# Linear attention with an MLP: far chunks' projections in small PE tiles, and a planner that counts a lead for each run of small operations

## The chip, the cores and the metric

The kernel runs on one core of one Trainium2 chip. The metric is the device time of one execution in microseconds; smaller is better. Three runs of the kernel before took 245.31, 246.84 and 247.11 us, so the median is 246.84 us.

## What is computed

Inputs are float32. The attention is linear: each head's query and key vector x (32 values) becomes 64 features, the products of all pairs of S1 x and S2 x. Its output, laid out as 4352 tokens of 128 values, goes through an MLP with 2048 hidden columns.

```python
def phi(x):
    a = np.einsum('rd,bhsd->bhsr', S1, x)
    b = np.einsum('rd,bhsd->bhsr', S2, x)
    return np.einsum('bhsi,bhsj->bhsij', a, b).reshape(*x.shape[:-1], r * r)
q_p, k_p = (phi(q), phi(k))
kv = np.einsum('bhsf,bhsd->bhfd', k_p, v)
z = np.sum(k_p, axis=2)
num = np.einsum('bhsf,bhfd->bhsd', q_p, kv)
den = np.einsum('bhsf,bhf->bhs', q_p, z)[..., None] + 1e-06
...
h = x @ w_in
g = h * np.clip(h + 3.0, 0.0, 6.0) / 6.0
out = g @ w_out
```

There are 4 batches, 4 heads, 1088 positions and r = 8.

## The kernel before, in words

The tokens are cut into eight chunks of 512 and a last one of 256 (CHUNKS), which gathers the last 64 positions of all batches. The hidden columns are cut into eight pairs of 128-column blocks (fp 0 to 7).

Keys (`keys`, `features`): for each batch two groups of tiles are projected on PE (abps_k, L530), copied by ACT (ab_k, L539) and multiplied to features by DVE and POOL (ph_k, L558). PE then sums features times values into one bank (kvps, L593), and ACT copies that to kvb (L618).

Queries: chunks 0 and 1 are the near ones and are turned by PE. Chunks 2 to 8 are the far ones (`far_queries`). Their projection (mm_far, L535, abps_q) takes two matmuls over 64 columns of weights each and writes one bank. DVE turns it in blocks of 32 (cp_far, L543), POOL makes the features (ph_q), DVE turns them (pht, L745), four DMAs write them to DRAM (phd, L751), and one reads them back with features across the partitions (phT, L756). PE multiplies by kvb (nd, L636) and DVE divides (L643 to L647). The result x is turned on its way through DRAM in the same manner (L773 to L782), and split into two halves xh and xl (L681, L685).

MLP: one step is a chunk c and a pair fp. h is the sum of three products for each of two blocks (L811, L812, L817), six matmuls of 512 columns. ACT makes relu (L825), DVE the gate (L828), ACT the upper half gh (L832) and POOL or DVE the lower half gl (L836). The output o is again six matmuls (L857, L858 from gh, L860 from gl). A matmul of 512 columns is called a slot below. h has two buffers, and a third step's h can be written only when the gate of the step two before has read its own. Weights come as 64-bit values and are converted in blocks of 512 columns (wi and wo 0 to 3, L371 to L396), seven steps of each on DVE.

What sets the order: each operation is entered in a `Plan` with its cost on each engine that can run it, a due time, its needs and its buffers. `Plan.order` walks through time, starts on each free engine the operation that is due first among those whose needs and buffers are there, and the instructions are emitted in that order. The due times come from the tables at the head (STEP, DUES, LAG, W_DUE, CONV_LEAD, LEADS). Each engine then executes its list in order and waits at an instruction whose needs are not there. While nothing is at hand before 17 us, fillers (warm, L354) are put in PE's list.

`bufs` of an operation are taken when it starts. Tag "a" stands for two banks that the far projections use:

```python
far_queries(c, xneed[c], ("a",), ("a",), both)
```

Of the kernel before, what the change touches and what calls it, by code (L numbers as in the profile page):

```python
# [23 lines left out]
HP = P // 2  # L24
Q = P // 4
# [8 lines left out]
AB = 2 * H * R  # L34
# [15 lines left out]
NEAR = 2  # L50
# [48 lines left out]

STEP = 5.06  # L100
DUES = (317.92, 316.34, 129.31, 384.08)
LAG = 128.57
W_DUE = (-152.92, 321.22, 23.24, 201.42, 251.62, 14.82, 266.57, 276.24)
CONV_LEAD = (-252.29, -232.94, 463.37, -221.73, 549.89, 31.5, 265.14, 219.73, 219.47)
LOAD_DUE = {}
LEADS = ({'ab': -466.98, 'cp': -244.73, 'ph': 113.36, 'kv': -102.29, 'kvb': -199.83, 'tr': -78.56, 'trcp': -30.35, 'nd': -572.11, 'norm': 297.56, 'xt': 543.02, 'xh': -868.0, 'xl': 204.57, 'k0': -407.3, 'kld': 146.8, 'vld': -256.29, 'qld': -79.85, 'rd': -154.99, 'xw': 402.82, 'xr': 513.46}, {'ab': 106.42, 'cp': 408.81, 'ph': 46.58, 'kv': 85.72, 'kvb': -43.81, 'tr': -441.07, 'trcp': -288.36, 'nd': -2.3, 'norm': -121.67, 'xt': 347.83, 'xh': 86.64, 'xl': 378.1, 'k0': 9.14, 'kld': 371.66, 'vld': 59.77, 'qld': 218.44, 'rd': 139.58, 'xw': 405.77, 'xr': 51.94}, {'ab': -161.26, 'cp': -355.61, 'ph': 225.14, 'kv': -82.13, 'kvb': 258.9, 'tr': -84.99, 'trcp': -282.18, 'nd': 9.09, 'norm': 441.52, 'xt': -380.46, 'xh': -96.54, 'xl': -168.68, 'k0': 149.54, 'kld': -6.91, 'vld': 496.37, 'qld': 447.25, 'rd': -88.95, 'xw': -359.0, 'xr': 167.27})


HOLD = 10.14
HOLD_DUE = -34.33  # L110
SOON = 0.51
SOON_DUE = 27.65
PATIENCE = 0.0
# [35 lines left out]
class Plan:  # L149
# [4 lines left out]

    def add(self, cost, due, deps, emit, bufs=(), cols=0, ready=0.0, moved=0.0, dual=False, recs=0):
        deps = [d for d in deps if d is not None]
        op = Op(cost, due, emit, list(bufs), cols, len(deps), ready, dual=dual, moved=moved, recs=recs)
        for d in deps:
            d.then.append(op)
        for b in op.bufs:  # L160
            b.left += 1
        self.ops.append(op)
        return op

    def fetched(self, t, recs):
# [32 lines left out]
    def choose(self, op, t, at, soon):  # L198
# [16 lines left out]
        return idle[0]  # L215

    def order(self):
        self.cols = {}
        self.port = 0.0
        self.begun, self.asked = 0, []  # L220
        self.moving = MOVING
# [6 lines left out]
        while left:  # L228
# [13 lines left out]
            for op in avail:  # L242
                if op.ready > t and len(op.cost) == 1 and all(b.held or any(free[g] for g in b.tags) for b in op.bufs):
                    soon[next(iter(op.cost))].append((op.ready, op.due))
            began = []
            for op in avail:
                if op.ready > t or not all(b.held or any(free[g] for g in b.tags) for b in op.bufs):
                    continue
# [77 lines left out]
def fused_kernel(ctx: ExitStack, tc: tile.TileContext, qT, kT, v1, sb, w_in, w_out, outT):  # L326
# [9 lines left out]
    def bank(tag, name):  # L336
        return psum[tag].tile([P, 512], F32, name=name, tag=tag)
# [179 lines left out]
    def features(src, n, name, tag, due, ld, srcb, psb, eng_cost, LEAD, far=False, w=HP):  # L517
# [4 lines left out]
        pb, abb, phb = Buf(psb), Buf(("ab",)), Buf((tag,))  # L522
        T["abb"], T["n"] = abb, n

# [35 lines left out]
        if far:  # L560
            o1 = plan.add({PE: 0.1 + 0.121 * n}, due - LEAD["ab"], [ld], mm_far, [srcb, pb, abb], 256 * n, S_READY, recs=8)
            o2 = plan.add({DVE: 0.12 + 0.067 * n}, due - LEAD["cp"], [o1], cp_far, [pb, abb])
        else:
            o1 = plan.add({PE: 0.13 + 0.115 * n if w == HP else 0.137 + 0.112 * n}, due - LEAD["ab"], [ld], mm, [srcb, pb, abb], 256 * n, S_READY, recs=8 * n if w == HP else 16 * n)
            o2 = plan.add({ACT: 0.06 + 0.0535 * n}, due - LEAD["cp"], [o1], cp, [pb, abb])
# [11 lines left out]
    def keys(b, due, psbs, ph_eng):  # L577
# [25 lines left out]
        for half in range(2):  # L603
# [20 lines left out]
    def divided(c, due, T, t, m, ready, phTb, nb, xb, LEAD):  # L624
# [102 lines left out]
    def far_queries(c, due, psb, ndb, ph_eng):  # L727
# [218 lines left out]
```

## Time and profile before

| what | us |
|---|---|
| median of 3 runs | 246.84 |
| lowest and highest | 245.31, 247.11 |
| the profiled execution | 244.85 |
| span of its instructions | 243.0 |
| PE busy in the span | 233.8 |
| DVE busy in the span | 184.7 |
| ACT busy in the span | 164.5 |
| POOL busy in the span | 154.1 |

The profile is of one execution, whose own time is 1.85 us longer than the span from its first to its last instruction. Times in the rows count from the start of the span. The records of matmuls overlap: a slot lasts about 0.39 us, but the next one starts earlier, so what a slot costs is read from starts. A float32 matmul leaves two records; 128*64 behind MATMUL is the size of the weights, the shape behind it is weights' or moving operand's as the profile names it. An x with a number counts records that follow each other.

### The profile page before, as it was taken

The page shows a single profiled execution, that of the slowest core. Times are in us where ns is not written, and L with a number is a line of the kernel's source. Part 1 is how long each engine was busy: PE and PEld are TensorE (multiplying, and loading weights), DVE is VectorE, ACT ScalarE, POOL GpSimd, SP SyncE. Part 2 cuts the span into 40 slices and gives each one's busy share as a digit, 9 for nine tenths or more (in the row PEclk, how much of TensorE's full clock was granted, in tenths as well). Part 3 has the DMA queues.
Part 4 walks back from the last instruction along what each step waited for, and adds up shares of the span by engine and source line. Part 5 has one row for each costly group of instructions (what it writes and reads, how often), then busy time and mean ns, then how long its engine had stood idle before and what let it go on. Part 6 is the DMA issues. An engine that isn't in the chain of part 4 may idle for free.

```text
span 243.0 us, 5464 instructions
## 1 busy us (share of the span) xinstructions
PE 233.8 (96%) x2214; PEld 182.2 (75%) x2214; DVE 184.7 (76%) x246; ACT 164.5 (68%) x205; POOL 154.1 (63%) x102
## 2 busy tenths in 40 slices
PE   8969789999999999999999899999999999999994
PEld 3757666787777778877878687777888878888894
DVE  2869999999899899788657756857648883747643
ACT  3455476888697648756766866849857875878571
POOL 2742867999699998474879844035663305867441
PEclk9999999999999999999999999999999999999999
DMA  6889973032037559704423000000100010001010
GB/s 206 263 282 386 373 249 115 1 88 87 4 87 184 180 146 295 239 0 136 127 89 86 18 29 20 25 0 3 43 0 0 0 43 3 0 0 46 0 43 22
DMA packets 18007, 23.80 MB, mean 98 GB/s; under 512 B 1728, under 2 KB 11072, under 8 KB 17984
## 3 DMA queue, kind: packets, MB, share of 16 engines
q1 hardware_dynamic: 17984, 23.48, 30.5%
q8 instruction: 17, 0.28, 0.5%
q14 instruction: 6, 0.05, 0.1%
HBM read 16.26 MB, written 7.21 MB: 97 GB/s over the span
## 4 chain that ended last, share of the span: by engine, by line
PE 86%; POOL 5%; issue 2%; DMA 2%; ACT 2%; DVE 1%; POOLq 0%; ACTq 0%
PE h L811 13%; PE o L857 13%; PE o L860 13%; PE h L817 12%; PE h L812 12%; PE o L858 12%; PE nd L636 3%; DMA woraw<-w_out_dram 2%; POOL gl L836 2%; PE warm L354 2%; PE kvps L593 2%; POOL ph_k L558 2%; PE abps_k L530 2%; PE abps_q L535 1%; PE xps L664 1%
## 5 line engine op out<-in xcount | busy, mean ns | idle before, releaser
L836 POOL TENSOR_TENSOR gl<-g,gh 128x1024 fp32r<-128x1024 f32 (+1 forms) x50 | 117.9, 2368 | 63.0 <-ACT gh L832 36.9
L828 DVE SCALAR_TENSOR_TENSOR g<-g,h 128x1024 f32<-128x1024 f32 (+1 forms) x72 | 82.9, 1156 | 24.7 <-ACT g L825 24.1
L825 ACT ACTIVATE g<-h 128x1024 f32<-128x1024 f32 (+1 forms) x72 | 70.3, 979 | 40.7 <-POOL gl L836 20.9
L832 ACT CAST gh<-g 128x1024 fp32r<-128x1024 f32 (+1 forms) x72 | 71.5, 1001 | 15.0 <-PE o L858 10.6
L811 PE MATMUL h<-xh,wi_hi 128*128 128x512 f32 (+1 forms) x148 | 56.8, 384 | 0.9 <-DVE g L828 0.9
L817 PE MATMUL h<-xl,wi_hi 128*128 128x512 f32 (+1 forms) x148 | 56.0, 378 | 0.0
L812 PE MATMUL h<-xh,wi_lo 128*128 128x512 f32 (+1 forms) x148 | 55.7, 376 | 0.0
L857 PE MATMUL o<-gh,wo_hi 128*128 128x512 f32 (+1 forms) x144 | 55.6, 389 | 0.0
L858 PE MATMUL o<-gh,wo_lo 128*128 128x512 f32 (+1 forms) x144 | 54.6, 382 | 0.0
L860 PE MATMUL o<-gl,wo_hi 128*128 128x512 f32 (+1 forms) x144 | 43.4, 385 | 0.0
L836 DVE TENSOR_TENSOR gl<-g,gh 128x1024 fp32r<-128x1024 f32 (+1 forms) x22 | 31.6, 1438 | 14.6 <-PE o L860 8.5
L811 PEld LDWEIGHTS h<-xh,wi_hi 128*128 128x128 f32 x148 | 27.7, 187 | 8.5 <-DVE g L828 1.3
L817 PEld LDWEIGHTS h<-xl,wi_hi 128*128 128x128 f32 x148 | 27.7, 187 | 5.9
L857 PEld LDWEIGHTS o<-gh,wo_hi 128*128 128x128 f32 x144 | 27.0, 188 | 6.7 <-issue 0.6
L812 PEld LDWEIGHTS h<-xh,wi_lo 128*128 128x128 f32 x148 | 27.8, 188 | 5.2
L858 PEld LDWEIGHTS o<-gh,wo_lo 128*128 128x128 f32 x144 | 27.0, 188 | 5.4
L860 PEld LDWEIGHTS o<-gl,wo_hi 128*128 128x128 f32 x144 | 25.8, 188 | 5.7 <-issue 0.4
L558 POOL TENSOR_TENSOR ph_k<-ab_k 128x512 f32<-128x512 f32 (+1 forms) x14 | 13.4, 978 | 10.9 <-ACT ab_k L539 10.9
L558 POOL TENSOR_TENSOR ph_q<-ab_q 128x512 f32<-128x512 f32 x15 | 15.8, 1073 | 0.9 <-ACT ab_q L539 0.5
L636 PEld LDWEIGHTS nd<-kvb,phT 128*32 128x32 f32 (+1 forms) x480 | 8.6, 113 | 4.0 <-issue 3.3
L593 PEld LDWEIGHTS kvps<-v,ph_k 128*32 128x32 f32 (+3 forms) x504 | 7.3, 113 | 5.4 <-issue 3.4
L593 PE MATMUL kvps<-v,ph_k 128*32 128x33 f32 (+3 forms) x504 | 8.8, 202 | 2.1 <-issue 1.6
(77 smaller groups left out, 165.8 us busy)
## 6 DMA issues: line engine op xcount, KB each, us to landing
phd<-pht SPq DMA_DIRECT2D x24, 128.0 KB, 3.9
phT<-phd SPq DMA_DIRECT2D x6, 512.0 KB, 4.4
wiraw<-w_in_dram SPq DMA_DIRECT2D x4, 512.0 KB, 5.5
qT<-qT_dram SPq DMA_DIRECT2D x8, 256.0 KB, 5.5
woraw<-w_out_dram SPq DMA_DIRECT2D x4, 512.0 KB, 5.4
outT_dram<-os SPq DMA_DIRECT2D x8, 256.0 KB, 2.0
xd<-xt SPq DMA_DIRECT2D x24, 64.0 KB, 1.8
xT<-xd SPq DMA_DIRECT2D x6, 256.0 KB, 2.7
```

Of the source, the lines that this page charges most:

```text
L558: engines[e].tensor_tensor(out, a_, b_, op=ALU.mult)
L593: nc.tensor.matmul(K["ps"][e : e + k, w], T["ph"][:rows, t, h * F + f : h * F + f + k], vbox[0][:rows, t, w], start=i == 0 and h < 2, stop ...
L811: nc.tensor.matmul(T["h"][:, u, i:j_], wi_hi[:, f], x, start=True, stop=False)
L812: nc.tensor.matmul(T["h"][:, u, i:j_], wi_lo[:, f], x, start=False, stop=False)
L817: nc.tensor.matmul(T["h"][:, u, i:j_], wi_hi[:, f], x, start=False, stop=True)
L825: nc.scalar.activation(T["g"][:, :, :n], T["h"][:, :, :n], AF.Relu, bias=3.0, scale=1.0)
L828: nc.vector.scalar_tensor_tensor(T["g"][:, :, :n], T["g"][:, :, :n], 6.0, T["h"][:, :, :n], op0=ALU.min, op1=ALU.mult)
L832: nc.scalar.copy(T["gh"][:, :, :n], T["g"][:, :, :n])
L836: engines[e].tensor_tensor(T["gl"][:, :, :n], T["g"][:, :, :n], T["gh"][:, :, :n].bitcast(F32), op=ALU.subtract)
L857: nc.tensor.matmul(o, wo_hi[:, f], T["gh"][:, u, :n], start=first and u == 0, stop=False)
L858: nc.tensor.matmul(o, wo_lo[:, f], T["gh"][:, u, :n], start=False, stop=False)
L860: nc.tensor.matmul(o, wo_hi[:, f], T["gl"][:, u, :n], start=False, stop=last and u == 1)
```

## The change

The far projection is done in eight matmuls instead of two. Each takes 64 rows (one pair of heads, p) and 32 columns of weights (that pair's), and moves a quarter g of the chunk's tokens, 128 columns. The eight tiles differ in their rows p and in the output partitions g, and the two pairs of heads write two different banks. So an operation now takes two banks of tag "a" at once, and `room` tests that two are free. DVE turns the two banks one after the other, each half as wide. Since the quarters lie otherwise in the features, each far chunk writes them with eight DMAs of half the size.

In the planner, small operations have a kind and a lead, which is counted once for a run of operations of one kind, and the costs of the small operations are lower by it. The tables of due times are all new, and with them the order of all engines. The cut diff:

```diff
-STEP = 5.06
-DUES = (317.92, 316.34, 129.31, 384.08)
+STEP = 4.32
+DUES = (370.39, 363.67, 175.22, 475.38)
...
+    lead: float = 0.0
+    kind: str = ""
...
+    def taken(self, op):
+
+        cost = op.cost[PE] + (op.lead if op.kind != self.last else 0.0)
+        self.last = op.kind
+        return cost
...
+    def room(op, free):
+
+        taken = []
+        for b in op.bufs:
+            if not b.held:
+                g = next((g for g in b.tags if free[g] > taken.count(g)), None)
+                if g is None:
+                    return False
+                taken.append(g)
+        return True
...
-                op.end = at[e] = self.run(self.fetched(t, op.recs), op.cost[e], op.cols) if e == PE else t + op.cost[e]
+                op.end = at[e] = self.run(self.fetched(t, op.recs), self.taken(op), op.cols) if e == PE else t + op.cost[e]
...
+        pbs = [pb, Buf(psb)]
...
         def mm_far(_):
-            T["ps"] = bank(pb.tag, f"abps_{name}")
-            for e in (0, HP):
-                nc.tensor.matmul(T["ps"][e : e + HP, : n * HP], s_sb, src[0][:, e * n : (e + HP) * n], start=True, stop=True)
+
+            T["pss"] = [bank(b.tag, f"abps_{name}_{p}") for p, b in enumerate(pbs)]
+            w = n * Q
+            for p, g in product(range(2), range(4)):
+                r = slice(p * HP, (p + 1) * HP)
+                nc.tensor.matmul(
+                    T["pss"][p][g * Q : (g + 1) * Q, :w],
+                    s_sb[r, p * Q : (p + 1) * Q],
+                    src[0][r, g * w : (g + 1) * w],
+                    start=True,
+                    stop=True,
+                    tile_position=(p * HP, g * Q),
+                )
...
         def cp_far(_):
             T["ab"] = buf("ab", [P, 5 * AB], f"ab_{name}")
-            nc.vector.transpose(T["ab"][:, : n * AB], T["ps"][:, : n * AB])
+            w = n * Q
+            for p in range(2):
+                nc.vector.transpose(T["ab"][:, p * w : (p + 1) * w], T["pss"][p][:, :w])
...
-            o1 = plan.add({PE: 0.1 + 0.121 * n}, due - LEAD["ab"], [ld], mm_far, [srcb, pb, abb], 256 * n, S_READY, recs=8)
-            o2 = plan.add({DVE: 0.12 + 0.067 * n}, due - LEAD["cp"], [o1], cp_far, [pb, abb])
+            o1 = plan.add({PE: 0.055 * n}, due - LEAD["ab"], [ld], mm_far, [srcb, *pbs, abb], 128 * n, S_READY, recs=32, lead=0.16, kind="far")
+            o2 = plan.add({DVE: 0.22 + 0.067 * n}, due - LEAD["cp"], [o1], cp_far, [*pbs, abb])
...
         def wr(_):
             d = dram.tile([2, 4, Q, n], F32, name=f"phd_{c}", tag=f"phd_{c}")
-            for e, p in product(range(2), range(2)):
-                k = (2 * e + p) * Q
-                nc.sync.dma_start(d[p, :, :, e * n // 2 : (e + 1) * n // 2].rearrange("f r x -> r f x"), T["turn"][k : k + Q])
+            w = n // 4
+            for g in range(4):
+                src = T["turn"][g * Q : (g + 1) * Q].rearrange("r f (p x) -> r f p x", p=2)
+                for p in range(2):
+                    nc.sync.dma_start(d[p, :, :, g * w : (g + 1) * w].rearrange("f r x -> r f x"), src[:, :, p])
...
-        a = plan.add({SP: 4 * ISSUE}, due - LEAD["trcp"], [a], wr, [turnb], moved=n * 1.024)
+        a = plan.add({SP: 8 * ISSUE}, due - LEAD["trcp"], [a], wr, [turnb], moved=n * 1.024)
```

The other small operations get lead and kind in the same manner (ab 0.135, kv 0.11, nd 0.135).

How the instructions move, at three places. Names: cva are conversion steps, wi1 is weight block 1, g_0_1 is the gate of chunk 0, pair 1.

DVE, before, around the first gates of the MLP:

```order
L396 TENSOR_TENSOR wi_lo_161<-rest_wi1_534,cva_wi1_448 128x512
L685 TENSOR_TENSOR xl_1_663<-xps_1_638,xh_1_662 128x512
L375 TENSOR_SCALAR cva_wo1_735<-woraw1_321 128x512
L828 SCALAR_TENSOR_TENSOR g_0_0_551<-g_0_0_551,h_0_0_433 128x1024
L378 SCALAR_TENSOR_TENSOR cva_wo1_735<-woraw1_321,cva_wo1_735 128x512
L543 STREAM_TRANSPOSE ab_q4_764<-abps_q4_739 128x256
L828 SCALAR_TENSOR_TENSOR g_0_1_692<-g_0_1_692,h_0_1_650 128x1024
```

and now:

```order
L397 TENSOR_SCALAR cva_wi2_694<-wiraw2_439 128x512
L397 TENSOR_SCALAR cva_wo1_701<-woraw1_322 128x512
L400 SCALAR_TENSOR_TENSOR cva_wi2_694<-wiraw2_439,cva_wi2_694 128x512
L400 SCALAR_TENSOR_TENSOR cva_wo1_701<-woraw1_322,cva_wo1_701 128x512
L864 SCALAR_TENSOR_TENSOR g_0_0_691<-g_0_0_691,h_0_0_649 128x1024
L406 TENSOR_SCALAR cva_wi2_694<-wiraw2_439 128x512
L592 TENSOR_TENSOR ph_k7_773<-abps_k7_669,ab_k7_703 128x256
L406 TENSOR_SCALAR cva_wo1_701<-woraw1_322 128x512
L409 SCALAR_TENSOR_TENSOR cva_wi2_694<-wiraw2_439,cva_wi2_694 128x512
L409 SCALAR_TENSOR_TENSOR cva_wo1_701<-woraw1_322,cva_wo1_701 128x512
L412 SCALAR_TENSOR_TENSOR wi_hi_160<-mag_wi2_652,cva_wi2_694 128x512
L864 SCALAR_TENSOR_TENSOR g_0_1_753<-g_0_1_753,h_0_1_698 128x1024
```

Ahead of the first gate there are now two conversion steps of two blocks each; between the first and the second gate stand six operations where two stood.

PE, before, from the end of h of chunk 0, pair 1, to the first product of chunk 1 (kvps_2: batch 2):

```order
L817 MATMUL h_0_1_650<-xl_0_426,wi_hi_160 128x256
L593 MATMUL kvps_2_674<-v_4_430,ph_k4_660 32x33 x16
L530 MATMUL abps_k5_695<-s_ab_157,kT_5_380 32x2x32 x20
L593 MATMUL kvps_2_674<-v_4_430,ph_k4_660 32x33 x16
L535 MATMUL abps_q4_739<-qT_4_401,s_sb_146 64x256 x2
L593 MATMUL kvps_2_674<-v_5_493,ph_k5_745 32x33 x8
L811 MATMUL h_1_0_761<-xh_1_662,wi_hi_160 128x512
L812 MATMUL h_1_0_761<-xh_1_662,wi_lo_161 128x512
```

and now:

```order
L847 MATMUL h_0_1_698<-xh_0_422,wi_hi_160 128x256
L848 MATMUL h_0_1_698<-xh_0_422,wi_lo_161 128x256
L853 MATMUL h_0_1_698<-xl_0_423,wi_hi_160 128x256
L627 MATMUL kvps_2_717<-v_4_510,ph_k4_647 32x33 x32
L627 MATMUL kvps_2_717<-v_5_394,ph_k5_584 32x33 x16
L847 MATMUL h_1_0_783<-xh_1_658,wi_hi_160 128x512
L848 MATMUL h_1_0_783<-xh_1_658,wi_lo_161 128x512
```

Between the two there is only kvps; the projections of k5 and of chunk 4 that stood there are elsewhere: k5 (and k7) ahead, chunk 4 behind.

PE, before, at a far projection:

```order
L817 MATMUL h_1_2_879<-xl_1_663,wi_hi_160 128x512
L860 MATMUL o_0_0_835<-gl_0_1_829,wo_hi_162 128x512 x2
L535 MATMUL abps_q6_895<-qT_6_628,s_sb_146 64x256 x2
L811 MATMUL h_1_3_899<-xh_1_662,wi_hi_160 128x512
L812 MATMUL h_1_3_899<-xh_1_662,wi_lo_161 128x512
```

and now, at another one:

```order
L848 MATMUL h_1_1_856<-xh_1_658,wi_lo_161 128x512
L560 MATMUL abps_q2_0_868<-qT_2_330,s_sb_146 32x128 x4
L560 MATMUL abps_q2_1_869<-qT_2_330,s_sb_146 32x128 x4
L853 MATMUL h_1_1_856<-xl_1_659,wi_hi_160 128x512
L896 MATMUL o_0_0_848<-gl_0_0_788,wo_hi_162 128x512 x2
L893 MATMUL o_0_0_848<-gh_0_1_853,wo_hi_162 128x512
```

Now each is eight matmuls in two banks, and it stands inside the six products of an h.

## Rows read from the trace of the kernel before

**Rows 1.** The page, busy us (share) xinstructions, and the granted clock by slice.
```profile
PE 233.8 (96%) x2214; PEld 182.2 (75%) x2214; DVE 184.7 (76%) x246; ACT 164.5 (68%) x205; POOL 154.1 (63%) x102
...
PEclk9999999999999999999999999999999999999999
```

**Rows 2.** Timeline of PE: start us, us, engine, line, operation; two slots, six apart.
```profile
128.20 0.39 PE L811 MATMUL h<-xh,wi_hi 128*128 128x512 f32 x1
...
129.60 0.39 PE L857 MATMUL o<-gh,wo_hi 128*128 128x512 f32 x1
```

**Rows 3.** Timeline of PE around the far projection of chunk 6.
```profile
42.90 0.63 PE L860 MATMUL o<-gl,wo_hi 128*128 128x512 f32 x2
43.46 0.65 PE L535 MATMUL abps_q<-qT,s_sb 128*64 128x256 f32 x4
...
44.38 0.39 PE L812 MATMUL h<-xh,wi_lo 128*128 128x512 f32 x1
```

**Rows 4.** Timeline of PE around the far projection of chunk 8 (half).
```profile
75.61 0.40 PE L817 MATMUL h<-xl,wi_hi 128*128 128x512 f32 x1
75.94 0.44 PE L535 MATMUL abps_q<-qT,s_sb 128*64 128x128 f32 x4
...
76.64 0.39 PE L858 MATMUL o<-gh,wo_lo 128*128 128x512 f32 x1
```

**Rows 5.** Timeline of PE around a run of nd.
```profile
168.13 0.63 PE L860 MATMUL o<-gl,wo_hi 128*128 128x512 f32 x2
168.69 0.67 PE L636 MATMUL nd<-kvb,phT 128*32 128x66 f32 x32
...
169.63 0.39 PE L858 MATMUL o<-gh,wo_lo 128*128 128x512 f32 x1
```

**Rows 6.** Timeline of PE around a run of kvps of batch 2.
```profile
34.97 0.40 PE L817 MATMUL h<-xl,wi_hi 128*128 128x512 f32 x1
35.30 0.89 PE L593 MATMUL kvps<-v,ph_k 128*32 128x33 f32 x64
...
36.46 0.39 PE L812 MATMUL h<-xh,wi_lo 128*128 128x512 f32 x1
```

**Rows 7.** Waits, whole span: us in total, times, longest us.
```profile
PE h L811 <- DVE g L828: 0.9, 1, 0.9
```

**Rows 8.** Timeline of DVE in the ramp [idle before, its releaser].
```profile
14.52 0.69 DVE L375 TENSOR_SCALAR cva_wo<-woraw 128x512 uint32<-128x512 uint32 x1 [2.09 <-DMA woraw<-w_out_dram]
...
19.47 0.42 DVE L685 TENSOR_TENSOR xl<-xps,xh 128x256 fp32r<-128x256 f32 x1 [0.19 <-PE xps L664]
...
28.78 0.69 DVE L558 TENSOR_TENSOR ph_k<-abps_k,ab_k 128x512 f32<-128x512 f32 x1 [0.39 <-ACT ab_k L539]
29.39 0.69 DVE L393 TENSOR_SCALAR cva_wi<-wi_hi 128x512 uint32<-128x512 uint32 x1
...
32.37 1.22 DVE L828 SCALAR_TENSOR_TENSOR g<-g,h 128x1024 f32<-128x1024 f32 x1
33.50 0.69 DVE L378 SCALAR_TENSOR_TENSOR cva_wo<-woraw,cva_wo 128x512 uint32<-128x512 uint32 x1
```

**Rows 9.** Timeline of PE: its longest wait, and the first product of chunk 1.
```profile
15.18 0.65 PE L530 MATMUL abps_k<-s_ab,kT 128*32 128x64 f32 x32 [1.80 <-ACT mag_wo L371]
...
33.73 0.47 PE L811 MATMUL h<-xh,wi_hi 128*128 128x512 f32 x1
```

**Rows 10.** Groups on DVE by form: busy us, mean ns of one | idle before.
```profile
L543 DVE STREAM_TRANSPOSE ab_q<-abps_q 128x256 f32<-128x256 f32 x6 | 2.7, 446 | 0.0
...
L543 DVE STREAM_TRANSPOSE ab_q<-abps_q 128x128 f32<-128x128 f32 x1 | 0.3, 301 | 0.0
```

**Rows 11.** Timeline of SP, and the DMA issues: KB each, median us to landing.
```profile
49.86 1.80 SPq L751 DMA_DIRECT2D phd<-pht  x4
...
phd<-pht SPq DMA_DIRECT2D x24, 128.0 KB, 3.9
phT<-phd SPq DMA_DIRECT2D x6, 512.0 KB, 4.4
```

More of the change, by code (lines that the diff above doesn't have):

```diff
@@ L97 @@
 SPLIT = 2
-STEP = 5.06
-DUES = (317.92, 316.34, 129.31, 384.08)
-LAG = 128.57
-W_DUE = (-152.92, 321.22, 23.24, 201.42, 251.62, 14.82, 266.57, 276.24)
-CONV_LEAD = (-252.29, -232.94, 463.37, -221.73, 549.89, 31.5, 265.14, 219.73, 219.47)
-LOAD_DUE = {}
[L106 to L113, printed above, removed]
+STEP = 4.32
+DUES = (370.39, 363.67, 175.22, 475.38)
+LAG = 133.32
+W_DUE = (-280.49, 231.08, -2.05, 212.68, 282.36, 65.09, 225.29, 271.1)
+CONV_LEAD = (-98.52, -269.14, 497.5, -209.44, 598.42, 4.56, 94.61, 172.23, 117.07)
+LOAD_DUE = {}
+LEADS = ({'ab': -441.49, 'cp': -249.6, 'ph': 96.71, 'kv': 42.02, 'kvb': -127.48, 'tr': -33.62, 'trcp': -32.52, 'nd': -816.0, 'norm': 382.87, 'xt': 864.13, 'xh': -878.34, 'xl': 273.47, 'k0': -365.56, 'kld': 42.89, 'vld': -245.02, 'qld': -185.29, 'rd': -182.12, 'xw': 461.04, 'xr': 397.68}, {'ab': 196.19, 'cp': 555.93, 'ph': -51.97, 'kv': 104.25, 'kvb': -111.02, 'tr': -429.63, 'trcp': -74.33, 'nd': -11.79, 'norm': -83.99, 'xt': 233.04, 'xh': 270.53, 'xl': 381.25, 'k0': -6.21, 'kld': 574.19, 'vld': 300.69, 'qld': 184.87, 'rd': -33.4, 'xw': 378.12, 'xr': -39.45}, {'ab': -60.83, 'cp': -293.22, 'ph': 144.23, 'kv': -36.19, 'kvb': 263.03, 'tr': -178.18, 'trcp': -158.4, 'nd': -24.58, 'norm': 518.21, 'xt': -294.29, 'xh': -137.22, 'xl': -218.45, 'k0': 55.04, 'kld': -30.98, 'vld': 652.39, 'qld': 342.93, 'rd': 3.77, 'xw': -356.84, 'xr': 299.14})
+HOLD = 14.88
+HOLD_DUE = 24.52
+SOON = 11.8
+SOON_DUE = 206.94
+PATIENCE = 0.96
 @dataclass(eq=False)
@@ L153, in __init__, with add @@
         self.ops = []
-    def add(self, cost, due, deps, emit, bufs=(), cols=0, ready=0.0, moved=0.0, dual=False, recs=0):
+    def add(self, cost, due, deps, emit, bufs=(), cols=0, ready=0.0, moved=0.0, dual=False, recs=0, lead=0.0, kind=""):
         deps = [d for d in deps if d is not None]
-        op = Op(cost, due, emit, list(bufs), cols, len(deps), ready, dual=dual, moved=moved, recs=recs)
+        op = Op(cost, due, emit, list(bufs), cols, len(deps), ready, dual=dual, moved=moved, recs=recs, lead=lead, kind=kind)
         for d in deps:
@@ L215, in choose @@
         return idle[0]
+    @staticmethod
+    def room(op, free):
[7 more added lines that the diff above has]
+        return True
     def order(self):
@@ L219, in order @@
         self.port = 0.0
-        self.begun, self.asked = 0, []
+        self.begun, self.asked, self.last = 0, [], ""
         self.moving = MOVING
@@ L242, in order @@
             for op in avail:
-                if op.ready > t and len(op.cost) == 1 and all(b.held or any(free[g] for g in b.tags) for b in op.bufs):
+                if op.ready > t and len(op.cost) == 1 and self.room(op, free):
                     soon[next(iter(op.cost))].append((op.ready, op.due))
@@ L246, in order @@
             for op in avail:
-                if op.ready > t or not all(b.held or any(free[g] for g in b.tags) for b in op.bufs):
+                if op.ready > t or not self.room(op, free):
                     continue
@@ L283, in order @@
                 op = Op({PE: 0.214}, 0.0, self.filler, [], 512, start=t, engine=PE, recs=2)
+                self.last = ""
                 op.end = at[PE] = self.run(self.fetched(t, 2), 0.214, 512)
@@ L522, in features @@
         pb, abb, phb = Buf(psb), Buf(("ab",)), Buf((tag,))
-        T["abb"], T["n"] = abb, n
+        pbs = [pb, Buf(psb)]
         def mm(_):
@@ L560, in features @@
         if far:
-            o1 = plan.add({PE: 0.1 + 0.121 * n}, due - LEAD["ab"], [ld], mm_far, [srcb, pb, abb], 256 * n, S_READY, recs=8)
-            o2 = plan.add({DVE: 0.12 + 0.067 * n}, due - LEAD["cp"], [o1], cp_far, [pb, abb])
+            o1 = plan.add({PE: 0.055 * n}, due - LEAD["ab"], [ld], mm_far, [srcb, *pbs, abb], 128 * n, S_READY, recs=32, lead=0.16, kind="far")
+            o2 = plan.add({DVE: 0.22 + 0.067 * n}, due - LEAD["cp"], [o1], cp_far, [*pbs, abb])
         else:
-            o1 = plan.add({PE: 0.13 + 0.115 * n if w == HP else 0.137 + 0.112 * n}, due - LEAD["ab"], [ld], mm, [srcb, pb, abb], 256 * n, S_READY, recs=8 * n if w == HP else 16 * n)
+            o1 = plan.add({PE: 0.115 * n if w == HP else 0.112 * n}, due - LEAD["ab"], [ld], mm, [srcb, pb, abb], 256 * n, S_READY, recs=8 * n if w == HP else 16 * n, lead=0.135, kind="ab")
             o2 = plan.add({ACT: 0.06 + 0.0535 * n}, due - LEAD["cp"], [o1], cp, [pb, abb])
@@ L611, in keys @@
                 i = t0 + t - b * KT
-                prev = plan.add({PE: 0.175 if KV_COLS[b] == Q else 0.26}, d - LEAD["kv"] + 0.3 * t, [o3[t], lv, prev], partial(kv, t=t, i=i, T=T, vbox=vbox), [phb, vb, kvbuf], 528, recs=32 if KV_COLS[b] == Q else 16)
+                prev = plan.add({PE: 0.15 if KV_COLS[b] == Q else 0.25}, d - LEAD["kv"] + 0.3 * t, [o3[t], lv, prev], partial(kv, t=t, i=i, T=T, vbox=vbox), [phb, vb, kvbuf], 528, recs=32 if KV_COLS[b] == Q else 16, lead=0.11, kind="kv")
         def halves(_):
@@ L649, in divided @@
         batches = range(batch_of(c0), batch_of(c0 + n - 1) + 1)
-        a = plan.add({PE: 0.1 + 0.26 * m if c < NEAR else 0.11 + 0.245 * m}, due - LEAD["nd"] - lag, [ready, *(o for b in batches for o in kv_done[b])], nd, [phTb, nb, xb], 528 * m, recs=16 * m if c < NEAR else 32 * m)
+        a = plan.add({PE: 0.25 * m if c < NEAR else 0.233 * m}, due - LEAD["nd"] - lag, [ready, *(o for b in batches for o in kv_done[b])], nd, [phTb, nb, xb], 528 * m, recs=16 * m if c < NEAR else 32 * m, lead=0.135, kind="nd")
         return plan.add({DVE: 0.56 + 0.1 * m}, due - LEAD["norm"] - lag, [a], norm, [nb, xb])
```

## The prediction

> **What bounds the kernel now.** I read the page's busy shares first, then the timeline of TensorE (PE), then that of VectorE (DVE) in the ramp, then the waits. PE is busy 96% of the span and its granted clock stays at nine tenths or more in every slice, which is the level of 2.4 GHz [rows 1], so the time is the sum of what stands in PE's list plus the few places where PE waits. Most of the list is 816 slots of 512 columns (8.5 chunks, 16 column blocks, six products each), 0.2333 us a slot: six of them from 128.20 to 129.60 [rows 2]. Between the slots stand runs of small products. A run costs its own columns and a fixed part: take the start of the second slot behind a run, less one slot, less the end of the last slot ahead of it. A far chunk's projection costs 0.78 (42.90 plus two slots is 43.37; 44.38 less a slot is 44.15), the half chunk's 0.56 [rows 3, 4]. The two differ by half a chunk, so a whole chunk's columns are 0.44 and the fixed part is 0.34. By the same reading a run of 32 records of nd costs 0.80, so 0.46 without the fixed part, 14.3 ns a record [rows 5], and a run of 64 records of kvps 1.02, so 10.6 ns a record [rows 6].
>
> As a check I add up before from slot 18, which ends at 35.20 [rows 6]. There follow 798 slots (186.2) and 19 runs: 6.4 fixed, nd 6.0, kvps 2.2, far 1.5, abps_k 1.0, in all 17.1. PE has one wait there, 0.85 for a DVE gate [rows 7], with some 0.2 to start again. That makes 239.6; the 3.4 us to the span's end of 243.0 are the last output and its store, which do not change.
>
> **The change part by part.**
> *The far projections.* Before, 4 records of 256 columns in tiles 64 columns wide; after, 16 records of 128 columns in tiles of 64 rows by 32 columns. No row has this shape. From below: one record alone streams at the rate of the old ones, 0.44/8 = 0.055 us, and eight tiles at once would make 16 of them 0.11. From above: no overlap at all makes 0.88. The nearest rows are those of tiles 32 columns wide: if a record costs what one of nd costs (14.3 ns), 0.23; if it grows with its columns as from kvps (33 columns, 10.6) to nd (66 columns, 14.3), 21 ns and 0.34; if it grows in proportion to nd's columns, 0.44, nothing gained. I take 0.28 for a whole chunk, the middle of the first two. With 6.5 chunks this is 0.16 x 6.5 = 1.0 us off PE; the ends are -2.1 and +2.9.
> The Trainium skill ("TensorEngine Tiling (Array Packing)", Key Properties) says that different tiles load weights and multiply in parallel. By that rule all eight tiles would run at once and the far sum would be 0.7 instead of 1.8. The 32-wide tiles of this trace do not show it: an nd record has 66 columns, which take 30 ns at the slot's rate, and comes every 14.3 ns, which is two at a time where four tiles are named.
>
> *The order of PE.* Behind the ramp there are fewer runs, since kvps of batches 2 and 3 stand together and nd of a chunk mostly stands in one run of 64. From the first slot of h_1_1 on, after has 16 runs: 5.4 fixed less 0.1 for the short transposes, nd 6.0, kvps 144 records 1.5, two leads inside the long run of kvps and far 0.2, far 6.5 x 0.28 = 1.8. Together 14.85.
>
> *The ramp.* Here DVE decides. h has two buffers, so the first product of chunk 1 (h_1_0) waits for the gate of h_0_0 on DVE. Before, DVE goes from 14.52 to that gate at 32.37 with only 0.19 and 0.39 of waiting [rows 8], so 17.27 of work. In the new order four things leave that stretch (half of ph_k2 0.60, two transposes 0.37 each, one half of ph_k4 0.60; a row of 0.69 is followed 0.60 later by the next, and a transpose of 0.45 [rows 10] 0.08 before its end likewise) and these come in: half of ph_k3 0.60, a ph_k5 of half that size 0.34, three more conversion steps 1.80. Net +0.80. I keep 0.3 of the 0.58 of waiting, since nd's rows on DVE now stand a little ahead of PE's nd. The gate then starts at 32.9, takes 1.13 to the next row [rows 8] and ends at 34.0, and h_1_0 starts about 34.2 (before 33.73 [rows 9]). PE has little left by then: behind kvps of batch 1, which I put at 23.7 (an estimate from the lengths of ph_k3's parts), stand abps_k4, the transposes, 24 half-width products, abps_k7 and 96 records of kvps, some 6.5 us. So PE waits from about 30.5, and everything that it has is queued behind the waiting product. The length of this wait does not enter the sum, which goes by DVE's rows. Next, h_1_0 takes 1.5, abps_k6 with the rest of kvps 1.4, four products of o 0.9: 38.1. Then h_1_1 needs the second gate, which now stands behind five conversion steps and a small ph_k7 (3.0 + 0.34): it starts at 37.4, ends at 38.5, and h_1_1 starts at 38.75. With 0.1 for the restart and 794 slots (185.2) the end is 38.85 + 185.2 + 14.85 = 238.9, against 239.6: **-0.7 us**. So the ramp gives back most of what the spared runs (19 against 16, with the 1.05 at 135) and the far tiles bring.
>
> *Later gates.* By the same count of DVE's rows the gates of chunk 1 end at 42.1, 44.5, 48.5 and 50.5, each just ahead of the product that needs its buffer; a far projection also needs both "a" banks free, and finds the previous one's transposes done 0.1 to 0.2 earlier. Cover is thin there, 0.1 to 0.5 a piece; where it goes, a miss costs a few tenths, and five of them 1 us.
>
> *The transposes.* One of 256 columns is 446 ns, one of 128 is 301 [rows 10]. Two instead of one add 0.16 for each chunk, or 0.08 if the second overlaps the first as above: 0.5 to 1.0 us of DVE in all. From chunk 2's on this is hidden under PE's list, where DVE has idle time; the ones before 50 us are in the gates above, at 0.6 a pair.
>
> *The writes.* Eight DMAs a chunk instead of four cost SP 3.6 us instead of 1.80 [rows 11]. Behind them on SP's queue stand a load of the last queries and the read of phT. From the turn at about 46.8: 3.6 to issue, 3.9 and 4.4 to land [rows 11], so phT is there at 58.7; nd of chunk 2 stands in PE's list at about 63.9. Cover 5 us; without it the cost would be 1.8, once. The list in the planner (leads, the room test for two banks) issues nothing by itself.
>
> **The sum.** 244.85 for the profiled execution, less 0.7, is 244.15. That execution is 0.8% under the median of the runs shown (246.84), so on the scale of that median I forecast **246.1**. About 1% (2.5 us) is what a measurement of this kernel can tell from no change.
>
> **Rivals.**
> *PE's clock falls in the new wait (slower).* In this trace the longest wait of PE is 1.80 us [rows 9] and no slice leaves 2.4 GHz. The new wait is about twice as long. If the clock drops to 1.2 GHz behind it, the 3.9 us of PE work from 34.2 to 38.1 take up to 7.8 (twice the length of the rows at 2.4 GHz); 0.6 of that is hidden by the second gate. So +0.6 to +3.3 on the sum: 246.7 to 249.4, and with the far tiles at 0.44 up to 250.5. It decides from the point where the drop lasts over some 2.5 us, and then it is slower by 1%. The Trainium skill ("TensorE: Matmul & The Clock Gate", Part 1) has the rule: an engine left idle goes back to half rate until it has been busy again. No run here shows where that begins. Against it: the kvps and h_0_1 just ahead of the wait are dense. Chance 0.14.
> *The far tiles do not overlap (slower).* 0.88 a chunk: 6.5 x 0.60 = +3.9, 250. For it: in the rows tiles 64 columns wide run one behind the other (0.44 for 4 x 256 columns). Against it: the 32-wide rows overlap by two. Chance 0.05.
> *Waits in the middle come back.* Before has 1.05 at 135, from a chain of POOL and ACT over the buffers of h, and the later order is all new. One or two such places: 247.2 to 248.3, no difference that can be told. Chance 0.22.
> *The far projections cost as before or the change does no more than reorder (0.44).* +1.0: 247.2. Chance 0.13.
> *Faster.* Eight tiles at once (another -1.1) with a ramp in which the gate comes 1 us sooner, because ph and conversion steps overlap better than my rows: 243.5 to 244.5. Chance 0.13.
> *The forecast:* 0.33, by itself 245 to 247.2.
>
> **How the numbers follow.** Faster by over 1% (under 244.4) is most of the fast rival and a little of the forecast through the spread of runs (245.31 to 247.11): 0.14. Slower by over 1% (over 249.3) is the non-overlapping case, half of the clock case, and a few hundredths of the middle waits: 0.15. The rest, 0.71, is within 1%. The range leaves about one in ten at either end: 243.8 to 249.3.
>
> **What would show it.** In the profile after: records of the far projections as runs of 16 that cost 0.5 to 0.7 with the fixed part; PE's longest wait, 3 to 4 us, ahead of h_1_0 near 34, ended by a DVE gate; h_1_1 near 38.8; hardly a wait of PE behind 40; the last product near 239. A granted clock under 1.00 in the slices from 30 to 42 us would prove the clock rival; far runs of 0.8 or more would break the first term; h_1_0 before 33 would break the ramp.

## The result, and the profile after

The changed kernel takes 247.81 us (median of 16 runs), the kernel before in the same session 246.11: ratio 1.0096, interval 1.0072 to 1.0119. It is slower by 1.0%, about what can be told from no change; the forecast was 0.3% faster. The profiled execution took 247.79 us (before 244.85), its span is 245.8 (before 243.0), and the last slot ends at 242.64 where before ends at 239.65: 2.99 us to explain.

The page after, as [rows 1]:

```profile
PE 234.0 (95%) x2300; PEld 184.3 (75%) x2300; DVE 186.3 (76%) x261; ACT 163.8 (67%) x205; POOL 141.4 (58%) x94
...
PEclk9998789999999999999999999999999999999999
```

PE's busy time is that of before (233.8); the span grew. The granted clock, full in every slice before, dips in slices 4 to 6, from 18 to 37 us, so the ramp comes first. The timeline of PE there (start, us, engine, line, operation, records [idle before and what ended it]), then a stop and a far run behind the ramp, as [rows 3]:

```profile
19.89 0.54 PE L552 MATMUL abps_k<-s_ab,kT 128*32 128x64 f32 x24 [0.97 <-DMA kT<-kT_dram]
21.85 1.44 PE L552 MATMUL abps_k<-s_ab,kT 128*32 128x64 f32 x56 [1.42 <-issue]
23.22 1.15 PE L670 MATMUL nd<-kvb,phT 128*64 128x66 f32 x16
24.30 0.99 PE L627 MATMUL kvps<-v,ph_k 128*32 128x33 f32 x55
28.21 0.53 PE L627 MATMUL kvps<-v,ph_k 128*32 128x33 f32 x25 [2.93 <-issue]
...
35.09 1.03 PE L627 MATMUL kvps<-v,ph_k 128*32 128x33 f32 x96
36.12 0.50 PE L847 MATMUL h<-xh,wi_hi 128*128 128x512 f32 x1
...
40.56 0.50 PE L847 MATMUL h<-xh,wi_hi 128*128 128x512 f32 x1
...
51.05 0.64 PE L627 MATMUL kvps<-v,ph_k 128*32 128x33 f32 x36 [0.94 <-issue]
...
64.09 0.40 PE L894 MATMUL o<-gh,wo_lo 128*128 128x512 f32 x1
64.41 0.45 PE L560 MATMUL abps_q<-qT,s_sb 64*32 64x128 f32 x16
64.79 0.73 PE L896 MATMUL o<-gl,wo_hi 128*128 128x512 f32 x2
```

The wait that I forecast (3 to 4 us ahead of h_1_0, ended by VectorE) is not there: PE works without a stop from 28.21 to h_1_0 at 36.12. Instead PE stops twice in the middle of a run whose inputs are all present, a run of 80 abps_k after 24 records and one of 80 kvps after 55. The releaser is "issue": PE waits for nothing that the profile shows. VectorE in the same stretch, as [rows 8]:

```profile
22.85 0.69 DVE L592 TENSOR_TENSOR ph_k<-abps_k,ab_k 128x512 f32<-128x512 f32 x1 [1.85 <-ACT ab_k L571]
24.41 0.17 DVE L677 TENSOR_SCALAR den<-nd 128x8 f32<-128x8 f32 x1 [0.87 <-PE nd L670]
...
30.07 0.69 DVE L592 TENSOR_TENSOR ph_k<-abps_k,ab_k 128x512 f32<-128x512 f32 x1 [0.89 <-ACT ab_k L571]
...
34.84 1.22 DVE L864 SCALAR_TENSOR_TENSOR g<-g,h 128x1024 f32<-128x1024 f32 x1
```

VectorE waits 3.61 us from 12.94 on, each time for what stands behind PE's stops (ab_k is ScalarE's copy of abps_k). Before, it waited 0.58 [rows 8]. The gate of h_0_0 starts at 34.84 (before 32.37).

Between the two stops, busy time and count of each engine, granted clock, DMA share, GB/s; and PE's instruction queue (packets, MB, share of 16 engines) in the quarter microseconds from 19.25 and from 25.50:

```profile
21.75:25.50 3.75, 3.44 (x127) 3.01 (x127) 1.71 (x5) 1.35 (x3) 2.60 (x3) 0.56 1.04 408
```

```profile
q8 instruction: 1, 0.02, 22.1%
q8 instruction: 1, 0.02, 26.1%
```

PE executes 127 matmuls and 127 weight loads between the stops, 254 instructions. The instruction queue moves one packet of 0.02 MB for each such block (18 packets, 0.29 MB in the whole span; 17 and 0.28 before). One packet begins at 19.25 to 19.50, and PE goes on at 21.85; the next begins at 25.50 to 25.75, and PE goes on at 28.21: 2.4 to 2.7 us each time. Meanwhile the data loads hold the DMA engines at 104% of the span between the stops. Before has the same stops, 0.82 and 0.74, at other places of its list, with packets at 18.50, 25.00 and 29.75. The prediction passed over these rows.

**Theory.** The supply of PE's instructions binds in the ramp. A block of some 254 comes by DMA, stands behind the data, and follows the one before it by about 6.4 us (21.85 to 28.21). A small product of 32-bit numbers is two records, each with a load. Counted from the start, the stops stand behind records 346 and 473 of PE's list here and behind 472 and 599 in before. What differs is the work that lies behind them: the last product of h_0_0 is record 546 here, behind two such ends, and record 388 in before, ahead of the first stop. Both planners already count such blocks (`fetched`, HELD, ASK, MORE, FETCH), with 4.6 us from asking for one to having it; the prediction passed over that too. **Rivals:** VectorE's order, as I forecast; late kT and v; the tiles, banks and writes; the clock, which fell.

### The profile page after: what moved, and what is told of

Read it like the earlier page. It is cut to its first block, busy times and chain, and to the rows that moved or that the text cites. A ratio compares the mean times of both kernels' runs of the same rounds, so it can differ in the third digit from the quotient of the medians.

```text
span 245.8 us, 5668 instructions
## 1 busy us (share of the span) xinstructions
PE 234.0 (95%) x2300; PEld 184.3 (75%) x2300; DVE 186.3 (76%) x261; ACT 163.8 (67%) x205; POOL 141.4 (58%) x94
## 4 chain that ended last, share of the span: by engine, by line
PE 55%; ACT 0%; issue 0%
PE o L896 9%; PE o L893 9%; PE o L894 9%; PE h L847 9%; PE h L848 9%; PE h L853 9%; PE nd L670 2%; ACT os L912 0%; PE xps L698 0%
## 5 line engine op out<-in xcount | busy, mean ns | idle before, releaser
L872 POOL TENSOR_TENSOR gl<-g,gh 128x1024 fp32r<-128x1024 f32 (+1 forms) x46 | 109.5, 2389 | 69.0 <-ACT gh L868 34.1
L847 PEld LDWEIGHTS h<-xh,wi_hi 128*128 128x128 f32 x148 | 28.3, 191 | 7.6 <-DVE g L864 1.4
L872 DVE TENSOR_TENSOR gl<-g,gh 128x1024 fp32r<-128x1024 f32 (+1 forms) x26 | 30.2, 1164 | 3.8 <-ACT gh L868 2.8
L853 PEld LDWEIGHTS h<-xl,wi_hi 128*128 128x128 f32 x148 | 28.2, 190 | 6.1 <-issue 0.6
L848 PEld LDWEIGHTS h<-xh,wi_lo 128*128 128x128 f32 x148 | 28.3, 191 | 5.4
L592 POOL TENSOR_TENSOR ph_k<-ab_k 128x512 f32<-128x512 f32 (+1 forms) x13 | 12.8, 1005 | 14.9 <-ACT ab_k L571 6.5
```

Source lines behind the costliest of these rows:

```text
L592: engines[e].tensor_tensor(out, a_, b_, op=ALU.mult)
L847: nc.tensor.matmul(T["h"][:, u, i:j_], wi_hi[:, f], x, start=True, stop=False)
L848: nc.tensor.matmul(T["h"][:, u, i:j_], wi_lo[:, f], x, start=False, stop=False)
L853: nc.tensor.matmul(T["h"][:, u, i:j_], wi_hi[:, f], x, start=False, stop=True)
L872: engines[e].tensor_tensor(T["gl"][:, :, :n], T["g"][:, :, :n], T["gh"][:, :, :n].bitcast(F32), op=ALU.subtract)
```

## The experiments

**1. The list without the tiles.** After, with the old code for far chunks:

```diff
-            for p, g in product(range(2), range(4)):
-                ... 64 rows by 32 columns, two banks
+            for e in (0, HP):
+                nc.tensor.matmul(T["ps"][e : e + HP, : n * HP], s_sb, src[0][:, e * n : (e + HP) * n], start=True, stop=True)
```

> The changed list on every engine, but each far chunk projected by the old code: two products 64 columns wide over all 128 rows into one bank, one transpose of 256 columns, four writes. Supply theory: after loses its time in the ramp, where PE stands 1.42 and 2.93 us in the middle of runs of small products with nothing to wait for but its own next instructions (records 344 and 469 of its list, a distance of 125); the far tiles, whose runs cost 0.57 in the trace of after against 0.78 in before, bring about 0.2 x 6.5 = 1.3 us. So this kernel keeps the stalls and loses the gain: far runs of about 0.78, the stalls of 1.4 and 2.9 within 0.5 us, and the time is 1.0 to 1.8 us above that of after, so a ratio of about 1.015 to before. Rival, the far tiles with their two banks, two transposes and eight writes cost the time: this kernel is as fast as before or faster, ratio 0.99 to 1.00.

Measured: 247.87 us, ratio 1.0099 (1.0061 to 1.0137). Its waits (us in total, times, longest):

```profile
PE kvps L615 <- issue: 3.3, 1, 3.3
...
PE abps_k L552 <- issue: 1.0, 1, 1.0
```

The ramp's loss belongs to the list, as the first theory says. But its second half failed: this kernel isn't slower than after. A far run costs 0.77 to 0.78 here and 0.56 to 0.58 there, yet the last slots are 0.1 us apart. Two places in after give most of the gain of 1.3 back. Its first far run costs 0.97: its loads wait for VectorE's ph_k and then, for the second bank, for wi_lo, a conversion step. And the third stop, 0.94 at 51.05, stands in kvps behind record 980; this kernel, with 12 records less for each far chunk, doesn't have it. On the other side its h_1_1 comes 0.4 later than after's (40.96), so some 0.3 us of the balance stays unplaced.

**2. Fewer instructions, the same list.** After, with batch 1's kvps and abps_k 64 columns wide:

```diff
-            k = KV_COLS[b]
+            k = HP if b in (1,) else KV_COLS[b]
-                for e in range(0, P, w):
+                v = HP if name in ('k2', 'k3') else w
+                for e in range(0, P, v):
```

> After, but kvps and abps_k of batch 1 in products 64 columns wide instead of 32: 72 + 18 matmuls in place of 144 + 36, the same result, the list unchanged. A run of kvps takes PE some 0.1 us longer per key tile, 0.9 in all, while 90 records with their weight loads leave the stretch from 19 to 32 us. Supply theory (a block of some 125 records takes 6.4 us to come in that stretch, 51 ns a record): the stall that was 2.93 at 28.2 shrinks below 1 us or goes, the gate of h_0_0 starts 1 to 2.5 us before the 34.84 of after, and the ratio to before falls from 1.0096 to between 0.998 and 1.005. Rival, VectorE's order in the ramp decides (more conversion steps ahead of the gate): the gate stays at 34.8 within 0.4, and the time is that of after or up to 0.9 above. Rival, the late loads of kT and v decide: same as the second.

(In records, of which a product has two: kvps 72 for 144, abps_k 36 for 72, so 108 left and not 90.) Measured: 245.12 us, ratio 0.9989 (0.9944 to 1.0035).

```profile
22.82 0.34 PE L671 MATMUL nd<-kvb,phT 128*64 128x66 f32 x4 [0.41 <-issue]
...
27.43 0.58 PE L848 MATMUL h<-xh,wi_hi 128*128 128x256 f32 x1 [1.13 <-DVE wo_lo L418]
```

```profile
32.66 1.21 DVE L865 SCALAR_TENSOR_TENSOR g<-g,h 128x1024 f32<-128x1024 f32 x1
```

One stop of 0.41 is left of the two, and h_0_0 now ends at record 435, ahead of the second block's end. PE now waits for VectorE, which works without a pause from 25 us on, and the gate comes 2.2 us sooner. The kvps cost PE more here, not less, VectorE and the loads have the same work, and PE's wait for kT is longer (1.6, in after 1.0), so both rivals fall. With most of the stops gone, VectorE decides. That the gate is near the 32.9 that I had summed is partly luck: VectorE's row begins 1.76 sooner than I took it (12.76 for 14.52), and it waits 1.78, not 0.3.

**3. Fewer bytes ahead of the block.** After, with three loads later:

```diff
+    late = ("qT_3", "qT_2", "qT_4")
...
+        if op.kind == "wiraw3":
+            for o in moved:
+                o.emit(o.engine)
```

> After with nothing moved but three loads of SP's list: qT of chunks 2, 3 and 4 (256 KB each), issued from 16.52 to 18.89 in after, stand behind the load of wiraw at 23.76; the lists of the four compute engines are word for word those of after. Supply theory, with the contention that the trace shows (the 16 KB packet of PE's instruction queue begins at 19.25 and at 25.5, 2.6 us ahead of the first matmul behind each stall, and stands behind data for some 4 us while the 16 DMA engines are 99 to 103% busy): 0.79 MB at 400 GB/s is 2.0 us of transfers less in front of it, so the two stalls of 1.42 and 2.93 shrink by 2 to 3 us in sum, the packet that began at 25.5 begins at 23.5 to 24.5, the gate of h_0_0 starts 1 to 2 us before 34.84, and the ratio is 1.000 to 1.006. Rival, how long a block takes has nothing to do with the data loads: stalls and gate stay within 0.4 us, ratio 1.007 to 1.012. Rival, VectorE's work decides: as the first rival.

Measured: 246.02 us, ratio 1.0028 (0.9990 to 1.0067). PE, then the instruction queue from 24.00:

```profile
21.86 0.99 PE L552 MATMUL abps_k<-s_ab,kT 128*32 128x64 f32 x56 [1.35 <-issue]
...
26.32 0.53 PE L627 MATMUL kvps<-v,ph_k 128*32 128x33 f32 x25 [1.62 <-issue]
```

```profile
q8 instruction: 1, 0.02, 25.4%
```

The granted clock in this run from 20 us on, in the columns of the row between the stops above:

```profile
20.00:25.00 5.00, 2.80 (x151) 2.34 (x152) 4.15 (x11) 1.24 (x3) 2.10 (x3) 1.00 1.01 382
```

All engines but SP run the same list, instruction by instruction. The packet begins at 24.0 instead of 25.5 and the stop shrinks from 2.93 to 1.62; the gate starts at 32.97. So the second stop depends on the data ahead of the block. The first stop hardly moved (1.35): the fall of 1.4 us in sum is under the 2 to 3 that I expected, since its packet was no earlier (19.50). The third stays too, at 0.91.

**4. More instructions.** Before, with 72 short products more:

```diff
+                    for _ in range(2 if name in ("k2", "k3") else 0):
+                        nc.tensor.matmul(out[e : e + w, :, :R], src[0][:, t * P + e : t * P + e + w], s_ab[:, :, 0, :], start=True, stop=True)
```

> Before, with 72 short matmuls more in the ramp: behind each of the 36 products of abps_k of batch 1 stand two that write 16 of its 64 columns again with the same values. Supply theory: 72 records with their weight loads are 0.58 of a block of 125, at some 50 ns a record 3.6 us; PE's slack in that stretch takes up to 1, so stalls called issue grow from 0.82 + 0.74 to some 3 to 4.5, and the time rises by 1.5 to 3.5 us (ratio 1.006 to 1.014). Rival, a record costs only its time on PE (10 to 14 ns in rows of kvps and nd): 0.7 to 1.0 us of PE, half of it in slack, ratio 1.000 to 1.004, and the issue waits stay under 2 in sum.

Measured: 251.37 us, ratio 1.0218 (1.0120 to 1.0316).

```profile
PE abps_k L530 <- issue: 3.1, 2, 2.7
...
PE kvps L595 <- issue: 0.7, 1, 0.7
```

The stops are 3.8 in sum, as expected, against 1.56; 0.38 of that stands at the head of a run and not at a block's end. The time is far above both expectations. I had counted 72 records where there are 144, and on PE they cost far more than 10 to 14 ns: the run of abps_k from 13.65 to 16.09 is 64 records longer than the 32 that stand in its place in before, and takes 2.44 us, not 0.65. So this run mixes both prices, and only the stops speak for the theory: 0.70 and 2.73, 128 records apart.

**5. The tiles without the list.** The planner's costs and tables of before, with the code of after for far chunks:

```diff
-            o1 = plan.add({PE: 0.1 + 0.121 * n}, due - LEAD["ab"], [ld], mm_far, [srcb, pb, abb], 256 * n, S_READY, recs=8)
+            o1 = plan.add({PE: 0.1 + 0.121 * n}, due - LEAD["ab"], [ld], mm_far, [srcb, *pbs, abb], 256 * n, S_READY, recs=8)
```

> Before with the far tiles alone: 16 records of 128 columns in tiles of 64 rows by 32 columns, two banks, two transposes, eight writes; costs and tables of the planner as before. The list is the same up to the second far projection; from there on, where a far projection finds no two banks free, it is put off, and so other things move too. If the far tiles cost what after shows, their runs come to 0.55 to 0.6 and bring 1.3 us on PE; the list, which no table was fitted to, may lose it: 0.99 to 1.02. Stalls of PE for nothing (issue) stay at those of before, 0.8 and 0.7, since nothing moves in the list ahead of 33 us. If instead the two banks or the eight writes have a price of their own, PE shows new waits for DVE's transposes ahead of far runs, or waits for phT ahead of nd of chunk 2.

Measured: 261.55 us, ratio 1.0632 (1.0534 to 1.0729).

```profile
PE h L837 <- DVE g L854: 9.3, 4, 5.2
PE kvps L617 <- issue: 2.4, 1, 2.4
```

Far runs alone cost 0.57 to 0.58, as expected; the time is far outside. The far projections are put off, the first to 49.8 us (before 23.9), and gates come late four times, once by 5.2. That the need for two banks at once did this, through the planner, is my reading; no run holds the list of before and changes the banks alone. I was also wrong on the list ahead of 33 us, since the first far projection of before stands at 24 us. This run prices a displaced list, not the tiles.

**6. Both remedies** (edits 2 and 3 together).

> Both of the edits that are to free PE's supply: batch 1 in products 64 columns wide (as in the run that came to 0.9989 with a gate at 32.66 and VectorE without a pause from 25 to 40 us) and qT of chunks 2 to 4 loaded behind wiraw. Supply theory: the supply no longer binds with the first edit alone, VectorE does, so the second adds little: gate at 32.2 to 32.7, last slot at 239.0 to 239.7, ratio 0.995 to 1.000. If stalls of the supply were still hidden under VectorE's work (0.41 at 22.82), the gate could come at 32.0 and the ratio 0.993.

Measured: 244.97 us, ratio 0.9995 (0.9960 to 1.0031), gate at 32.15, last slot at 239.2: by the ratios the second edit adds nothing that can be told, as expected.

```profile
PE nd L671 <- issue: 1.2, 1, 1.2
```

But the supply still binds a little, which I had not expected: the stop is longer than run 2's (0.41), and VectorE waits 1.05 behind it. The gate comes 0.5 sooner all the same, since VectorE waits 1.3 in all and not 1.8.

**7. A list with other figures for the supply.** After with batch 1 in wider products, its planner's figures of blocks set anew and its tables fitted anew:

```diff
-HELD = 440
-ASK = 200
-MORE = 240
-FETCH = 4.6
+HELD = 436
+ASK = 186
+MORE = 250
+FETCH = 6.7
-            t = max(t, self.asked[(need - 1) // MORE] + FETCH)
+            a = self.asked[(need - 1) // MORE]
+            t = max(t, a + (FETCH if a < 26 else 4.5 if a < 32 else 3.0))
-KEY_COLS = (HP, Q, Q, Q)
-KV_COLS = (HP, Q, Q, Q)
+KEY_COLS = (HP, HP, Q, Q)
+KV_COLS = (HP, HP, Q, Q)
```

> A version meant to beat both: the code of after with batch 1 in products 64 columns wide, the planner's figures for PE's instruction blocks set to what the runs showed (500 records of both kinds, so 250 matmuls and loads a block; 6.7 us from asking to having one while the data loads run, 4.5 and 3.0 later, in place of 4.6 throughout), and its tables of due times and leads fitted anew to that. Supply theory: a list that knows the supply has no stall called issue over 0.5 us behind 14 us, and the ramp ends 2 to 5 us earlier than in after (first product of h_1_1 at 35.5 to 38.5 where after has 40.56); the tiles bring what they bring: ratio 0.980 to 0.997. If the supply was only a part, and VectorE's conversion steps hold the ramp whatever the list, the ratio is 0.997 to 1.003.

(A block is 254 instructions of both kinds in the traces; the 500 above is twice that, MORE in the diff is 250.) Measured: 241.96 us, ratio 0.9867 (0.9816 to 0.9918), better than both kernels. No stop called issue is over 0.2 us; among its waits:

```profile
PE abps_k L553 <- DMA kT<-kT_dram: 1.3, 3, 0.7
PE abps_k L553 <- DVE ph_k L593: 1.1, 1, 1.1
...
PE h L848 <- DVE g L865: 0.8, 1, 0.8
...
PE warm L377 <- issue: 0.2, 1, 0.2
```

**8. A second set of tables**, of nearly the same merit to the planner, and its profile:

> The same with other tables of nearly the same merit by the planner's own count: as the run beside it, within 0.5%. If the two differ by more than that, what decides is something the planner doesn't count.

> The second set of tables again, for its profile alone, since it came out 1.8% above the first by the ratios to before although the planner counts them alike. Supply theory: its list has a stall called issue of 1 us or more that the first does not have. Otherwise waits for VectorE's gates or for a bank of the far tiles: then the planner's missing term lies there.

Measured: 246.69 us, ratio 1.0045 (1.0011 to 1.0080).

```profile
PE h L848 <- DVE g L865: 2.6, 2, 1.5
PE abps_k L553 <- DMA kT<-kT_dram: 2.3, 3, 1.3
PE kvps L628 <- issue: 0.8, 1, 0.8
```

The two sets differ by 1.8%, not by under 0.5%, so this expectation failed. A stop of 0.8 has come back (under the 1 us that I looked for), but late gates and late kT weigh more. So the figures of the supply aren't enough for a good list; which of the planner's terms is missing stays open, and part of the gain of run 7 may be luck with its tables.

**9. The tiles' worth in the good list.** Run 7 with the old far projections (the edit of run 1):

> The refitted kernel that came to 0.9867 (0.9816 to 0.9918), its list unchanged, with the far projections of before: two products 64 columns wide over all 128 rows, one bank, one transpose, four writes. In the refitted trace six far runs cost 0.557 to 0.577 and the half chunk's 0.453, and none waits; before they cost 0.78 and 0.56. So if the tiles are worth what their rows say once nothing else gives it back, this kernel is 6 x 0.21 + 0.11 = 1.4 us slower, 0.57%: ratio to before 0.992, and its last slot 1.2 to 1.5 us later than the 237.2 + 0.4 of the refitted one. Rival, other waits take the place (as between after and its twin with the old tiles, 0.0): the two agree within 0.3 us in their last slots.

Measured: 243.97 us, ratio 0.9965 (0.9937 to 0.9993), 1.0% above run 7. Far runs cost 0.77 to 0.78 (run 7: 0.56 to 0.58), the half chunk's 0.56 (0.45), and the last slot comes 1.0 us later. Six runs by 0.20 and 0.11 make 1.3. Slot by slot the traces show it: this kernel falls back by 0.2 at each of the six and by 0.12 at the half one. Its last slot is 1.0 later and not 1.3 because it also enters the first far run 0.6 later and regains 0.9 from 82 to 84 us, where run 7 alone waits for xh and xl. The ratios' difference, 2.4 us, is wider, with intervals that reach down to 0.5, and the ratio is above the 0.992 that I expected. So the tiles bring their rows on PE; how much of that reaches the time isn't settled.

## Why the prediction was wrong

The time lies in the range (243.8 to 249.3), the sign is wrong. By the prediction's own steps:

- *Far projections*, 0.62 a run with the fixed part: measured 0.57 (16 records in 0.23), the low end of the two rows between which I chose. Right, with another 0.05 a run on our side. The trace agrees in part with the Trainium skill ("TensorEngine Tiling (Array Packing)", Key Properties), by which different tiles multiply in parallel: nearly four at a time (0.88 us without overlap, done in 0.23), not eight.
- *The banks*: "cover is thin there, 0.1 to 0.5 a piece". The first far run paid 0.4, in part to a conversion step, which I had not counted among the users of a bank.
- *The transposes and the writes*: 0.29 us a transpose of 128 columns, and the writes land in 2.2 us where four took 3.9. Neither shows in a wait of PE.
- *The ramp*, the step that failed: **"I keep 0.3 of the 0.58 of waiting"**, and with it "PE has little left by then". VectorE's work from 12.94 to the gate is 18.3 us, nearly as I had counted (17.27 + 0.80 = 18.07), and it even began 1.58 earlier. But it waited 3.61, for products that PE had no instructions for. The gate came at 34.84, not 32.9, h_1_0 at 36.12, not 34.2, and h_1_1 at 40.56, not 38.75: 1.8 of the error of 3.7 us. My count had PE finish 6.5 us of work and wait at 30.5, without counting records; PE worked until 36.12. "Here DVE decides" holds for its work: with the order of after it is 18.1 to 18.4 us in runs 1, 2, 3 and 6 as well. Only its waits differ, 3.8, 1.8, 2.1 and 1.3 us, and the gates follow them: 34.88, 32.66, 32.97 and 32.15.
- *Where the stops stand.* In before, after and runs 1 to 6 and 8 every stop of PE called issue of over 0.2 us, but for the 0.38 of run 4, stands behind record 343 of PE's list or a multiple of 127 records further (470, 597, 851, 978; to within 3), whether abps_k, nd or kvps is there. So it is the count that stops PE, and not an operand.
- *The order behind the ramp*, 14.85 and 0.1 from h_1_1 on: measured 242.64 − 40.56 − 794 × 0.2333 = 16.8. Of the 1.9 too much, 0.94 is the third stop, 0.4 the bank and 0.33 a gate at 106.9; the far tiles give 0.3 back; 0.5 I can't place.
- *The clock rival*: by the sign that I had named, under 1.00 from 30 to 42 us, it came true in part:

```profile
30.00:35.00 5.00, 5.00 (x67) 4.73 (x65) 4.93 (x9) 3.22 (x6) 1.08 (x1) 0.75 0.52 174
```

  From 30.1 to 32.5 the mean is 0.51, the level of 1.2 GHz, and the products of h_0_0 follow each other by 0.21 there, by 0.12 at full clock. Between the two stops it was 0.56: abps_k took 1.44 there and 0.99 in run 3 at 1.00. But the stops don't come from it. In runs 1 and 3 the clock is 1.00 from 20 to 25 us, and PE stops there all the same, until the block comes; run 1's gate is as late as after's. And from 30.07 to the gate VectorE works without a pause, so the slow products of h_0_0 are hidden.

The rule to weigh was in the Trainium skill ("Runtime: NRT & Kernel Launch", Instruction fetch mechanics): instructions come in blocks of 16 KiB, 256 of them, over a DMA queue of their own, while the block before runs. The trace agrees (254 instructions, packets of 0.02 MB). The page calls the cost of a boundary mostly hidden; here it was 0.9 to 2.9 us three times, so the measurement decides. In these traces it is hidden where 254 instructions last longer than a block takes to come: a slot is two instructions in 0.2333 us, so 127 slots last 29.6 us, and there is no stop behind 52.

## What to carry to other kernels

An idle time called issue, in the middle of a run of small products, at a fixed count of instructions, was a missing instruction block here. Before packing small products into a stretch that is also full of loads, count the instructions (matmuls, their passes and their loads) against the blocks that can arrive, check at which count the product stands that the next stage waits for, and whether wider tiles with fewer records come out ahead. A freed term on the busiest engine is worth its rows only if the list around it doesn't give it back: measure the new code in the old list and the old code in the new one.

## What was not expected of the hardware

- A block of 254 instructions followed the one before it by 6.4 us while data loads held the DMA engines at 104%, and PE went on 2.1 to 2.7 us after its packet began to move; with 0.79 MB of data less ahead of it the block came 1.9 us sooner.
- A record that writes only 16 columns cost about 28 ns on PE in run 4, (2.44 − 0.65) / 64, and one of 64 columns 20 ns (0.65 / 32). The short ones go to the same tile as the product ahead of them, and so may overlap less; that wasn't tried apart.
- Two of run 8's twelve executions took 1254.6 us. In the trace of one, slots follow each other by 1.28 us throughout instead of 0.2333, while VectorE's gates take the usual 1.16 and the granted clock reads 1.00. No run here shows why.
